# Keys split once per pair of heads and placed by DMA, query additions on GpSimd, in an attention and two-layer MLP kernel

## The chip, the cores and the metric

The kernel runs on one core of a Trainium2 chip. Such a core has five engines that run side by side, each with its own instruction queue that is worked off in order: TensorE (PE in the rows; its weight loads stand apart as PEld), VectorE (DVE), ScalarE (ACT), GpSimd (POOL) and SyncE (SP), which here issues every DMA transfer. The metric is the time of one execution in microseconds (us). A row of the profile that says L396 means line 396 of the kernel before.

## The reference, cut to what matters

```
q, k, v: (4, 8, 1152, 64) float32; w_in (512, 2048), w_out (2048, 512), a second pair likewise, float64
q_pool = q.reshape(B, H, S // 2, 2, D).mean(axis=3)
scores = q_pool @ k.T / sqrt(D);  scores -= max(scores, axis=-1)
attn = exp(scores);  attn /= sum(attn, axis=-1) + 1e-9
x = (attn @ v), heads side by side            # (2304, 512)
x = (h * cos(h)) @ w_out   with h = x @ w_in
out = elu(x @ w2_in) @ w2_out                 # (2304, 512) float32
```

## The kernel before, in words

**Exact products.** The kernel keeps float32's accuracy on a TensorE that rounds an operand of type float32r to 12 significant bits. An operand is split into hi (its rounding) and lo (what is left), and a product is made of several float32r products that accumulate in PSUM. Some products are done as plain float32 instead, which the trace records as two matmuls.

**Order of the work.** Attention goes over 16 pairs of heads (4 batches of 4 pairs). Head by head, `main_steps` (L429) makes 18 steps: 2 halves of 288 pooled queries by 9 blocks of 128 keys; so a pair has 36 steps. In a step, `s_step` (L438) makes the scores of one block by two matmuls (L442, L444) into one of three PSUM buffers `ps`, and ACT makes the exponentials `e` (L447, seven buffers). For 5 of the 9 key blocks (the tuple SPLIT) `halves` (L454) splits `e` one step later: hi is `eh` (a copy on ACT, L459, or on DVE, L457, in the first ten steps of the pair's first head), lo is `el` (a subtraction, L460, on GpSimd, and on DVE for steps 4 and 8 of the first head). Seven steps later (LAG) `v_step` (L464) multiplies by the values: three float32r matmuls (L475 to L477) for a split block, one float32 product (L479) for another. The values have 64 columns and a column of ones that gives the sum; their tiles `vt` and `vh` are 128 columns wide, the rest ones too.

**What is prepared for the next pair** while a pair is worked on, at steps that a hand-written plan fixes (L586 to L619):
- `add_q` (L319): five DVE additions pool the queries, steps 0 to 5. The squares (L308) that bound the rounding error are six ACT passes, steps 0 to 7.
- `q_group` (L323), at steps 4 and 6, and `k_group` (L347), at steps 8, 10 and 12: TensorE transposes (L332, L355) put both heads of the pair into one PSUM tile, head 0 on partitions 0 to 63 and head 1 on 64 to 127. One step later ACT copies each head's 64 partitions to hi (L337, L360), and two steps later DVE subtracts them to lo (L341, L364) and GpSimd copies hi once more (L343, L366). For the keys, hi goes to partitions 0 to 63 of `kst` of each head, lo to its partitions 64 to 127, and the second copy of hi to `k2`.
- `unit` (L383): from step 15 to 35, 27 units multiply the rounded queries by `kst` (L389, 384 keys at a time, through three PSUM buffers `big`), and DVE reduces each to its maximum (L396). `combine` (L398) and `spread` (L413) make the maxima that the score product then subtracts.
- Loads for the pair after (L250, step 12), values (L274, step 8; split at step 20 by L283), and decoding of the float64 weights, some 25 small tasks per pair on DVE, ACT and GpSimd (L117 to L132, far in the queues from one another), with a fetch and a store by DMA per half chunk.

Every engine takes its instructions in the order in which this plan writes them. In pairs 0 and 1 some units of the second head stand in other steps (L576 to L586). After attention come the two layers of the MLP (L647 on), which the change doesn't touch.

The ordering of one step, as the loop writes it:

```
s_step(i)
for t in due.pop(now[0], []): t()          # what later(steps, task) put off to this step
...                                        # v_step of seven steps ago
for t in plan.get(si, []): t()             # the plan's tasks of this step
```

Of the kernel before, what the change touches and what calls it, by code (L numbers as in the profile page):

```python
# [10 lines left out]
F32 = mybir.dt.float32  # L11
F32R = mybir.dt.float32r
# [18 lines left out]
EHV = 10  # L31
ELV = (4, 8)
# [3 lines left out]
def network(ctx, tc, q, k, v, w_in1, w_out1, w_in2, w_out2, out, ident, sq, exact):  # L36
    """Everything from inputs to output. The maxima that the softmax subtracts: from two exact
    products per score (exact), or from one that rounds the queries to 12 significant bits; sq then
    gets the sums of the squares of queries and keys, which bound what that rounding can do."""
# [20 lines left out]
    NM = 2 * NQB if exact else NQB  # L60

# [15 lines left out]
    # ------------------------------------------------- weights: float64 bits to hi + lo  # L77
# [8 lines left out]
    def decode_tasks(layer, f, half, dst):  # L86
        """Operations that bring half a chunk of weights (0: w_in, 1: w_out) into dst's hi and lo."""
# [78 lines left out]
    # ------------------------------------------------- blocks of tokens for the layers  # L166
# [52 lines left out]
    # ---------------------------------------------------------------- attention  # L219
    def attention():  # L220
# [5 lines left out]
        wd_p = att.enter_context(tc.tile_pool(name="wd", bufs=2))  # L226
        ps_big = att.enter_context(tc.tile_pool(name="ps_big", bufs=3, space=bass.MemoryType.PSUM))
# [6 lines left out]
        vhs = [apool.tile([P, 2 * NS, P], F32R, name=f"vh{i}") for i in range(2)]  # L234
        vls = [apool.tile([P, 2 * NS, D], F32R, name=f"vl{i}") for i in range(2)]
        for t in vts:
            nc.vector.memset(t[:, :, D:P], 1.0)
        for t in vhs:
            nc.gpsimd.memset(t[:, :, D:P].bitcast(F32), 1.0)
# [53 lines left out]
        def prep_tasks(n):  # L293
            kr, qr = raws.pop(n)
            qp = spool.tile([P, NQB, 2, D], F32, tag="qp", name=f"qp{n}")
# [12 lines left out]
            def square(i):  # L308
                x, m = (kr[:, 3 * i:3 * i + 3], P) if i < 3 else (qp[:, 2 * i - 6:min(2 * i - 4, NQB)], P)
                if i == 5:  # L310
                    m = SQ % P
                    x = x[0:m]
                junk = x_p.tile([P, KD, NB], F32, tag="xin", name=f"junk{n}_{i}")[:, 0, :].rearrange("p (c j d) -> p c j d", j=2, d=D)
                nc.scalar.activation(
                    junk[0:m, 0:x.shape[1]], x, AF.Square, accum_out=sq[0:m, i // 3, n, i % 3:i % 3 + 1])

            squares = [lambda i=i: square(i) for i in range(6)]
# [5 lines left out]
            def q_group(i0, i1):  # L323
                w = min(SQ, i1 * P) - i0 * P
                cols = [slice(j * OFF + i0 * P, j * OFF + i0 * P + w) for j in range(2)]
                ps = {}

                def put(pool=ps_big, tag="big"):
                    ps[0] = pool.tile([P, 512], F32, tag=tag, name=f"pq{n}_{i0}")
                    for i in range(i0, i1):  # L330
                        m = min(P, SQ - i * P)
                        nc.tensor.transpose(  # L332
                            ps[0][:, (i - i0) * P:(i - i0) * P + m],
                            qp[0:m, i].rearrange("p j d -> p (j d)"), ident[0:m, 0:m])

                def high(j):
                    nc.scalar.copy(qst[j][0:D, cols[j]], ps[0][j * D:(j + 1) * D, 0:w])  # L337

                def low(j):
                    hi = qst[j][0:D, cols[j]].bitcast(F32)  # L340
                    nc.vector.tensor_tensor(  # L341
                        q2[j][0:D, cols[j]], ps[0][j * D:(j + 1) * D, 0:w], hi, ALU.subtract)
                    nc.gpsimd.tensor_scalar(qst[j][D:P, cols[j]], hi, 1.0, 0.0, ALU.mult, ALU.add)  # L343

                return put, high, low

            def k_group(c0, c1):  # L347
                w = (c1 - c0) * P
                cols = slice(c0 * P, c1 * P)
                ps = {}  # L350

                def put():
                    ps[0] = ps_big.tile([P, 512], F32, tag="big", name=f"pk{n}_{c0}")
                    for c in range(c0, c1):
                        nc.tensor.transpose(  # L355
                            ps[0][:, (c - c0) * P:(c - c0 + 1) * P],
                            kr[:, c].rearrange("p j d -> p (j d)"), ident)

                def high(j):
                    nc.scalar.copy(kst[j][0:D, cols], ps[0][j * D:(j + 1) * D, 0:w])  # L360

                def low(j):
                    hi = kst[j][0:D, cols].bitcast(F32)
                    nc.vector.tensor_tensor(  # L364
                        kst[j][D:P, cols], ps[0][j * D:(j + 1) * D, 0:w], hi, ALU.subtract)
                    nc.gpsimd.tensor_scalar(k2[j][0:D, cols], hi, 1.0, 0.0, ALU.mult, ALU.add)  # L366

                return put, high, low

            adds = [lambda i=i: add_q(i) for i in range(NQB)]  # L370
            q_groups = [q_group(i, min(NQB, i + 3)) for i in range(0, NQB, 3)]
            k_groups = [k_group(c, c + NC // NU) for c in range(0, NC, NC // NU)]
            return adds, q_groups, k_groups, squares
# [55 lines left out]
        def main_steps(h):  # L429
# [8 lines left out]
            def s_step(i):  # L438
# [10 lines left out]
                if c in SPLIT:  # L449
                    eh = xs_p.tile([P, NB], F32R, tag="xh", name=f"eh{h}_{i}")[:, 0:HALF]  # L450
                    el = xs_p.tile([P, NB], F32R, tag="xl", name=f"el{h}_{i}")[:, 0:HALF]
                    es[i] = (eh, el)

                    def halves():  # L454
                        # The scalar engine has the next pair's copies in the first head's steps.
                        if j == 0 and i < EHV:
                            nc.vector.tensor_copy(eh, e)  # L457
                        else:
                            nc.scalar.copy(eh, e)  # L459
                        (nc.vector if j == 0 and i in ELV else nc.gpsimd).tensor_tensor(el, e, eh.bitcast(F32), ALU.subtract)  # L460

                    later(1, halves)

            def v_step(i):  # L464
# [6 lines left out]
                if c in SPLIT:  # L471
# [3 lines left out]
                    nc.tensor.matmul(acc[:, 0:HALF], vh, eh, start=first, stop=False)  # L475
                    nc.tensor.matmul(acc[0:D, 0:HALF], vl, eh, start=False, stop=False)  # L476
                    nc.tensor.matmul(acc[:, 0:HALF], vh, el, start=False, stop=last)  # L477
                else:
                    nc.tensor.matmul(  # L479
                        acc[:, 0:HALF], vt[:, j * NC + c, :], *e, start=first, stop=last)  # L480
# [43 lines left out]
        def group(g):  # L524
            put, high, low = g
            put()
            for j in range(2):
                later(1, lambda j=j: high(j))
                later(2, lambda j=j: low(j))
# [9 lines left out]
        for _, high, low in q_groups:  # L539
            high(0)  # L540
            low(0)
# [280 lines left out]
```

## Time and profile before

| | us |
|---|---|
| runs of the kernel before | 1426.86, 1427.74, 1429.59 |
| their median | 1427.74 |
| profiled execution, first to last instruction (span) | 1430.4 |
| of it ahead of the first step of attention | 15.1 |
| of it attention, to the last step | 594 |
| of it the MLP | 821 |

The page gives the profiled execution's span alone; no separate time for that execution is given, so its own time is at least 1430.4 us. A busy engine in a row is the union of its instructions' durations; a matmul's duration runs to its modelled end, so neighbouring matmuls overlap and a PE that shows as busy all the time can still be waiting a little. PEclk is the granted share of TensorE's clock: 1.00 is 2.4 GHz, 0.5 is 1.2 GHz.

### The profile page before, as it was taken

The page shows a single profiled execution, that of the slowest core. Times are in us where ns is not written, and L with a number is a line of the kernel's source. Part 1 is how long each engine was busy: PE and PEld are TensorE (multiplying, and loading weights), DVE is VectorE, ACT ScalarE, POOL GpSimd, SP SyncE. Part 2 cuts the span into 40 slices and gives each one's busy share as a digit, 9 for nine tenths or more (in the row PEclk, how much of TensorE's full clock was granted, in tenths as well). Part 3 has the DMA queues.
Part 4 walks back from the last instruction along what each step waited for, and adds up shares of the span by engine and source line. Part 5 has one row for each costly group of instructions (what it writes and reads, how often), then busy time and mean ns, then how long its engine had stood idle before and what let it go on. Part 6 is the DMA issues. An engine that isn't in the chain of part 4 may idle for free.

```text
span 1430.4 us, 22786 instructions
## 1 busy us (share of the span) xinstructions
PE 1368.7 (96%) x7683; PEld 1259.3 (88%) x7683; DVE 923.4 (65%) x1707; ACT 822.3 (57%) x2061; POOL 705.5 (49%) x849
## 2 busy tenths in 40 slices
PE   7998999999998999999999999999999999999997
PEld 5887888788887888899999999999999999999996
DVE  7789999999998999723888888887411111121111
ACT  5776777777776777655555555555633334343332
POOL 5657878777776787722222223232333333333332
PEclk8999999999999999999999999999999999999999
DMA  4232334445444443383525243439801010101000
GB/s 115 61 96 61 100 89 117 118 128 137 118 117 118 118 119 86 111 285 148 155 89 184 89 155 118 155 120 363 311 1 45 1 44 0 45 0 45 1 23 25
DMA packets 152542, 150.69 MB, mean 105 GB/s; under 512 B 81472, under 2 KB 129600, under 8 KB 152416
## 3 DMA queue, kind: packets, MB, share of 16 engines
q1 hardware_dynamic: 152416, 149.15, 34.4%
q8 instruction: 62, 1.02, 0.3%
q14 instruction: 64, 0.52, 0.1%
HBM read 105.46 MB, written 43.66 MB: 104 GB/s over the span
## 4 chain that ended last, share of the span: by engine, by line
PE 57%; issue 18%; DVE 15%; POOL 7%; ACT 2%; DMA 1%; SPq 0%; POOLq 0%; DVEq 0%; ACTq 0%
PE po L726 17%; PE ph L672 6%; PE ph L670 6%; PE ph L671 6%; POOL gl L702 6%; PE acc L479 5%; DVE mm L396 5%; PE pm L389 4%; PE ps L442 3%; PE ps L444 3%; PE acc L477 2%; PE acc L475 2%; PE acc L476 2%; DVE kst L364 1%; DVE e L128 1%
## 5 line engine op out<-in xcount | busy, mean ns | idle before, releaser
L702 POOL TENSOR_TENSOR gl<-u,gh 128x384 fp32r<-128x384 f32 x192 | 208.1, 1084 | 330.8 <-ACT gh L701 316.8
L460 POOL TENSOR_TENSOR el<-e,eh 128x288 fp32r<-128x288 f32 x288 | 253.1, 886 | 146.5 <-ACT eh L459 49.9
L447 ACT ACTIVATE e<-ps 128x288 f32<-128x288 f32 x576 | 234.2, 411 | 139.5 <-PE ps L444 97.7
L672 PE MATMUL ph<-xh,w 128*128 128x384 f32 x768 | 257.9, 336 | 0.0
L670 PE MATMUL ph<-xh,w 128*128 128x384 f32 x768 | 257.7, 336 | 0.0
L671 PE MATMUL ph<-xl,w 128*128 128x384 f32 x768 | 257.5, 335 | 0.0
L396 DVE TENSOR_REDUCE mm<-pm 128x1 f32<-128x384 f32 x432 | 221.3, 548 | 25.8 <-PE pm L389 24.6
L726 PE MATMUL po<-gh,w 128*128 128x384 f32 x768 | 211.5, 336 | 0.4 <-ACT gh L701 0.4
L389 PE MATMUL pm<-kst,qst 128*128 128x384 f32 x480 | 176.5, 415 | 27.6 <-DVE kst L364 15.4
L442 PE MATMUL ps<-qst,kst 128*128 128x288 f32 x576 | 197.1, 342 | 1.8 <-ACT e L447 1.8
L699 DVE SCALAR_TENSOR_TENSOR u<-ph,a 128x384 f32<-128x384 f32 x96 | 52.8, 554 | 225.7 <-POOL a L685 225.7
L726 PE MATMUL po<-w,gh 128*128 128x512 f32 x576 | 179.6, 393 | 0.0
L444 PE MATMUL ps<-q,k 69*128 69x288 f32 x576 | 174.3, 303 | 0.4 <-DVE q L418 0.4
L683 ACT ACTIVATE a<-ph 128x384 f32<-128x384 f32 x96 | 47.2, 492 | 213.9 <-PE ph L672 213.9
L479 PE MATMUL acc<-e,vt 128*128 128x288 f32 x512 | 169.4, 412 | 0.0
L701 ACT CAST gh<-u 128x384 fp32r<-128x384 f32 x192 | 97.4, 508 | 112.3 <-DVE u L696 86.9
L685 POOL TENSOR_SCALAR a<-a 128x384 f32<-128x384 f32 x96 | 49.4, 514 | 222.0 <-ACT a L684 222.0
L670 PEld LDWEIGHTS ph<-xh,w 128*128 128x128 f32 x768 | 144.2, 188 | 4.1
L671 PEld LDWEIGHTS ph<-xl,w 128*128 128x128 f32 x768 | 144.2, 188 | 3.9
L672 PEld LDWEIGHTS ph<-xh,w 128*128 128x128 f32 x768 | 144.2, 188 | 0.0
L389 PEld LDWEIGHTS pm<-kst,qst 128*128 128x128 f32 x480 | 90.3, 196 | 58.4 <-DVE mm L396 24.6
L726 PEld LDWEIGHTS po<-gh,w 128*128 128x128 f32 x768 | 140.2, 188 | 1.4 <-ACT gh L701 1.0
(87 smaller groups left out, 2779.0 us busy)
## 6 DMA issues: line engine op xcount, KB each, us to landing
w_d<-wd SPq DMA_DIRECT2D x56, 512.0 KB, 2.9
w<-w_d SPq DMA_DIRECT2D x56, 512.0 KB, 8.8
raw<-in_moe_w_in_dram SPq DMA_DIRECT2D x32, 512.0 KB, 5.3
raw<-in_moe_w_out_dram SPq DMA_DIRECT2D x32, 512.0 KB, 4.3
vt<-in_v_dram SPq DMA_DIRECT2D x32, 288.0 KB, 4.5
kr<-in_k_dram SPq DMA_DIRECT2D x30, 288.0 KB, 4.3
qr<-in_q_dram SPq DMA_DIRECT2D x32, 256.0 KB, 4.5
x_d<-xo SPq DMA_DIRECT2D x32, 144.0 KB, 2.3
```

The costliest lines, as they stand in the source:

```text
L389: nc.tensor.matmul(ps[:, 0:W], qst[:, i * P:(i + 1) * P], kst[:, u * W:(u + 1) * W], start=first, stop=last and not exact)
L396: nc.vector.reduce_max(mm[:, x, u:u + 1], ps[:, 0:W], axis=AX.X)
L442: nc.tensor.matmul(ps[:, 0:HALF], kst[:, c * P:(c + 1) * P], qst[:, qs], start=True, stop=False)
L444: nc.tensor.matmul(ps[:, 0:HALF], k2[0:KR, c * P:(c + 1) * P], q2[0:KR, qs], start=False, stop=True)
L447: nc.scalar.activation(e, ps[:, 0:HALF], AF.Exp, scale=SCALE)
L460: (nc.vector if j == 0 and i in ELV else nc.gpsimd).tensor_tensor(el, e, eh.bitcast(F32), ALU.subtract)
L479: nc.tensor.matmul(acc[:, 0:HALF], vt[:, j * NC + c, :], *e, start=first, stop=last)
L670: nc.tensor.matmul(h, wh, xh, start=(c == 0), stop=False)
L671: nc.tensor.matmul(h, wh, xl, start=False, stop=False)
L672: nc.tensor.matmul(h, wl, xh, start=False, stop=(c == KD - 1))
L702: nc.gpsimd.tensor_tensor(gl, u, gh.bitcast(F32), ALU.subtract)
L726: nc.tensor.matmul(o, a, b_, start=st and t == 0, stop=sp and t == 2)
```

## The change

The keys of pairs 1 to 15 are split once for both heads: ACT copies all 128 partitions of the transposed PSUM tile to a tile `uk`, DVE subtracts to `vk`, and ten DMA transfers per pair (64 partitions each) place the halves in `kst` and `k2` of the two heads; GpSimd's copies to `k2` go. Pair 0 keeps the old way but with both heads' copies ahead of the first step. The query additions go to GpSimd, in two instructions. The squares are three passes. All copies to `eh` are on ACT and all subtractions to `el` on GpSimd. The key groups stand at steps 0, 2 and 4, the query groups at 6 and 8, the transfers at steps 3 and 4 (first third of the keys, four transfers of 96 KB), 7 and 8 (the other two thirds, four of 192 KB) and 10 and 11 (`k2`, two of 288 KB), the load of the pair after at step 13. In pair 0 all of these stand seven steps later. The tiles of the values are 66 columns wide.

```
-        vts = [apool.tile([P, 2 * NC, P], F32, name=f"vt{i}") for i in range(2)]
+        vts = [apool.tile([P, 2 * NC, VW], F32, name=f"vt{i}") for i in range(2)]      # VW = D + 2
...
+            uk = upool.tile([P, S], F32R, tag="uk", name=f"uk{n}")
+            vk = upool.tile([P, S], F32R, tag="vk", name=f"vk{n}")
...
-                x, m = (kr[:, 3 * i:3 * i + 3], P) if i < 3 else (qp[:, 2 * i - 6:min(2 * i - 4, NQB)], P)
+                x, m = ((kr, P), (qp[:, 0:SQ // P], P), (qp[0:SQ % P, SQ // P:], SQ % P))[i]
...
-            def add_q(i):
-                m = min(P, SQ - i * P)
-                nc.vector.tensor_tensor(qp[0:m, i], qr[0:m, i, :, 0], qr[0:m, i, :, 1], ALU.add)
+            def add_q(i0, i1):
+                m = min(P, SQ - i0 * P)
+                nc.gpsimd.tensor_tensor(
+                    qp[0:m, i0:i1], qr[0:m, i0:i1, :, 0], qr[0:m, i0:i1, :, 1], ALU.add)
+
+            def place(dst, src):
+                nc.sync.dma_start(out=dst.bitcast(F32), in_=src.bitcast(F32))
...
+                def high():
+                    if n and tag == "k":
+                        nc.scalar.copy(uk[:, cols], ps[0][:, 0:w])
+                        return
+                    for j in range(2):
+                        dst = kst[j][0:D, cols] if tag == "k" else qst[j][0:D, j * OFF + c0:j * OFF + c0 + w]
+                        nc.scalar.copy(dst, ps[0][j * D:(j + 1) * D, 0:w])
+
+                def low():
+                    if n and tag == "k":
+                        nc.vector.tensor_tensor(vk[:, cols], ps[0][:, 0:w], uk[:, cols].bitcast(F32), ALU.subtract)
+                        return
+                    for j in range(2):
...
+                        nc.vector.tensor_tensor(lo, ps[0][j * D:(j + 1) * D, 0:w], hi.bitcast(F32), ALU.subtract)
+                        nc.gpsimd.tensor_scalar(again, hi.bitcast(F32), 1.0, 0.0, ALU.mult, ALU.add)
...
+            places = [
+                [lambda j=j, r=r, c=c: place(kst[j][halves[r], c], (uk, vk)[r][halves[j], c])
+                 for r in range(2) for j in range(2)] for c in (first, others)
+            ] + [[lambda j=j: place(k2[j][0:D, :], uk[halves[j], :]) for j in range(2)]] if n else []
...
                     def halves():
-                        # The scalar engine has the next pair's copies in the first head's steps.
-                        if j == 0 and i < EHV:
-                            nc.vector.tensor_copy(eh, e)
-                        else:
-                            nc.scalar.copy(eh, e)
-                        (nc.vector if j == 0 and i in ELV else nc.gpsimd).tensor_tensor(el, e, eh.bitcast(F32), ALU.subtract)
+                        nc.scalar.copy(eh, e)
+                        nc.gpsimd.tensor_tensor(el, e, eh.bitcast(F32), ALU.subtract)
...
-                    nc.tensor.matmul(acc[:, 0:HALF], vh, eh, start=first, stop=False)
+                    nc.tensor.matmul(acc[0:VW, 0:HALF], vh, eh, start=first, stop=False)
...
         for _, high, low in q_groups:
-            high(0)
-            low(0)
+            high()
+            low()
...
-                spread_over(d, d + 5, adds)
+                spread_over(d, d + 2, adds)
...
-                    at(d + 12, lambda: load(n + 2))
-                for x, g in enumerate(q_groups):
-                    at(d + 4 + 2 * x, lambda g=g: group(g))
-                for x, g in enumerate(k_groups):
-                    at(d + 8 + 2 * x, lambda g=g: group(g))
+                    at(d + 13, lambda: load(n + 2))
+                for x, g in enumerate(k_groups + q_groups):
+                    at(d + 2 * x, lambda g=g: group(g))
+                for x, step in enumerate((3, 7, 10)):
+                    spread_over(d + step, d + step + 2, places[x])
```

## Rows read from the trace of the kernel before

**Rows 1.** The page: busy time, share of the span and instructions of each engine.
```profile
PE 1368.7 (96%) x7683; PEld 1259.3 (88%) x7683; DVE 923.4 (65%) x1707; ACT 822.3 (57%) x2061; POOL 705.5 (49%) x849
```
**Rows 2.** Windows (busy time of each engine in a stretch): pairs 2 to 13, pair 15.
```profile
core 0: us, PE busy (x) PEld busy (x) DVE busy (x) ACT busy (x) POOL busy (x), PEclk, DMA share, GB/s
...
92.35:542.50 450.15, 416.96 (x2523) 368.38 (x2521) 422.00 (x823) 333.38 (x965) 346.88 (x417) 0.98 0.42 113
...
580.20:609.26 29.06, 27.28 (x166) 24.15 (x165) 17.76 (x31) 20.70 (x58) 21.86 (x22) 0.94 0.17 53
```
**Rows 3.** Windows over steps 0 to 6 of pairs 2 to 13: fastest, sum.
```profile
133.77:139.75 5.98, 5.98 (x40) 5.24 (x39) 5.60 (x16) 5.50 (x20) 4.05 (x5) 1.00 0.03 9
...
sum 82.68, PE 75.55 PEld 63.33 DVE 80.42 ACT 70.07 POOL 59.04; mean PE 6.30 PEld 5.28 DVE 6.70 ACT 5.84 POOL 4.92
```
**Rows 4.** Windows over steps 7 to 14 of the same pairs: sum.
```profile
sum 79.28, PE 79.25 PEld 72.63 DVE 74.40 ACT 75.41 POOL 57.21; mean PE 6.60 PEld 6.05 DVE 6.20 ACT 6.28 POOL 4.77
```
**Rows 5.** Windows over steps 15 to 21 of the same pairs: two pairs, sum.
```profile
221.22:230.13 8.91, 7.99 (x47) 6.85 (x45) 8.49 (x17) 5.14 (x16) 8.78 (x11) 1.00 0.99 243
...
330.99:339.35 8.36, 7.71 (x47) 6.70 (x45) 7.55 (x14) 4.79 (x14) 8.30 (x11) 1.00 0.62 153
...
sum 120.12, PE 101.12 PEld 85.88 DVE 109.47 ACT 75.66 POOL 108.49; mean PE 8.43 PEld 7.16 DVE 9.12 ACT 6.30 POOL 9.04
```
**Rows 6.** Windows over steps 22 to 35 of the same pairs: fastest, sum.
```profile
230.13:242.98 12.85, 12.85 (x85) 12.16 (x84) 12.16 (x25) 10.03 (x29) 11.40 (x13) 1.00 0.28 91
...
sum 168.07, PE 161.04 PEld 146.54 DVE 157.70 ACT 112.24 POOL 122.14; mean PE 13.42 PEld 12.21 DVE 13.14 ACT 9.35 POOL 10.18
```
**Rows 7.** Waits in pairs 2 to 13: us in total, times, longest us.
```profile
ACT e L447 <- POOL el L460: 25.3, 27, 2.0
...
PEld pm L389 <- DVE mm L396: 20.8, 32, 2.8
...
PE pm L389 <- DVE kst L364: 12.2, 15, 2.0
PEld pq L332 <- DVE qp L321: 10.1, 13, 1.7
```
**Rows 8.** Groups by line and shape: count, busy us, mean ns, idle before.
```profile
L460 POOL TENSOR_TENSOR el<-e,eh 128x288 fp32r<-128x288 f32 x288 | 253.1, 886 | 146.5 <-ACT eh L459 49.9 <-DVE eh L457 44.3 <-PE ps L444 26.3
...
L459 ACT CAST eh<-e 128x288 fp32r<-128x288 f32 x224 | 95.3, 425 | 0.0
...
L364 DVE TENSOR_TENSOR kst<-pk,kst 64x384 fp32r<-64x384 f32 x96 | 53.2, 556 | 7.1 <-ACT kst L360 4.8
...
L366 POOL TENSOR_SCALAR k<-kst 64x384 fp32r<-64x384 f32 x96 | 49.8, 532 | 3.4 <-ACT kst L360 2.5
...
L360 ACT CAST kst<-pk 64x384 fp32r<-64x384 f32 x96 | 45.0, 471 | 2.3 <-PE pk L355 1.2
...
L457 DVE CAST eh<-e 128x288 fp32r<-128x288 f32 x96 | 43.4, 452 | 0.5
...
L130 POOL TENSOR_TENSOR m<-m,wd 128x512 f32<-128x512 f32 x24 | 33.0, 1377 | 0.2
...
L321 DVE TENSOR_TENSOR qp<-qr 128x128 f32<-128x128 f32 x64 | 24.6, 396 | 1.9 <-DMA qr<-in_q_dram 1.8
...
L460 DVE TENSOR_TENSOR el<-e,eh 128x288 fp32r<-128x288 f32 x32 | 20.6, 644 | 1.1
```
**Rows 9.** Timeline of DVE ahead of the first steps: start us, us, instructions merged.
```profile
16.97 1.51 DVE L364 TENSOR_TENSOR kst<-pk,kst 64x384 fp32r<-64x384 f32 x3
```
**Rows 10.** Timeline of SP in pair 8 (one transfer's issue), and times to landing.
```profile
326.00 0.50 SPq L486 DMA_DIRECT2D x_d<-xo  x1
...
w<-w_d SPq DMA_DIRECT2D x56, 512.0 KB, 8.8
...
x_d<-xo SPq DMA_DIRECT2D x32, 144.0 KB, 2.3
```
**Rows 11.** Waits of SP's queue in pairs 2 to 13: total, times, longest.
```profile
SPq L152 <- POOL wd L131: 84.2, 18, 7.8
```

More of the change, by code (lines that the diff above doesn't have):

```diff
@@ L30 @@
 SV = 20
-EHV = 10
-ELV = (4, 8)
 @with_exitstack
@@ L60, in network @@
     NM = 2 * NQB if exact else NQB
+    VW = D + 2
     wpool = ctx.enter_context(tc.tile_pool(name="wpool", bufs=NPREW))
@@ L226, in attention @@
         wd_p = att.enter_context(tc.tile_pool(name="wd", bufs=2))
+        upool = att.enter_context(tc.tile_pool(name="upool", bufs=1))
         ps_big = att.enter_context(tc.tile_pool(name="ps_big", bufs=3, space=bass.MemoryType.PSUM))
@@ L229, in attention @@
         ps_a = att.enter_context(tc.tile_pool(name="ps_a", bufs=2, space=bass.MemoryType.PSUM))
-        vts = [apool.tile([P, 2 * NC, P], F32, name=f"vt{i}") for i in range(2)]
+        vts = [apool.tile([P, 2 * NC, VW], F32, name=f"vt{i}") for i in range(2)]
         k2s = [apool.tile([P, S], F32R, name=f"k2_{i}") for i in range(4)]
         qsts = [apool.tile([P, NQB * P], F32R, name=f"qst{i}") for i in range(4)]
-        vhs = [apool.tile([P, 2 * NS, P], F32R, name=f"vh{i}") for i in range(2)]
+        vhs = [apool.tile([P, 2 * NS, VW], F32R, name=f"vh{i}") for i in range(2)]
         vls = [apool.tile([P, 2 * NS, D], F32R, name=f"vl{i}") for i in range(2)]
         for t in vts:
-            nc.vector.memset(t[:, :, D:P], 1.0)
+            nc.vector.memset(t[:, :, D:VW], 1.0)
         for t in vhs:
-            nc.gpsimd.memset(t[:, :, D:P].bitcast(F32), 1.0)
+            nc.gpsimd.memset(t[:, :, D:VW].bitcast(F32), 1.0)
         for t in k2s:
@@ L317, in prep_tasks @@
-            squares = [lambda i=i: square(i) for i in range(6)]
-            def add_q(i):
-                m = min(P, SQ - i * P)
-                nc.vector.tensor_tensor(qp[0:m, i], qr[0:m, i, :, 0], qr[0:m, i, :, 1], ALU.add)
-            def q_group(i0, i1):
-                w = min(SQ, i1 * P) - i0 * P
-                cols = [slice(j * OFF + i0 * P, j * OFF + i0 * P + w) for j in range(2)]
+                x, m = ((kr, P), (qp[:, 0:SQ // P], P), (qp[0:SQ % P, SQ // P:], SQ % P))[i]
+                if not m:
+                    return
@@ new lines, in square @@
+                junk = x_p.tile([P, KD, NB], F32, tag="xin", name=f"junk{n}_{i}").rearrange("p c n -> p (c n)")
+                junk = junk[0:m, 0:x.shape[1] * 2 * D].rearrange("p (c j d) -> p c j d", j=2, d=D)
+                nc.scalar.activation(
+                    junk, x, AF.Square, accum_out=sq[0:m, min(i, 1), n, i // 2:i // 2 + 1])
+            squares = [lambda i=i: square(i) for i in range(3)]
+            def add_q(i0, i1):
+                m = min(P, SQ - i0 * P)
+                nc.gpsimd.tensor_tensor(
+                    qp[0:m, i0:i1], qr[0:m, i0:i1, :, 0], qr[0:m, i0:i1, :, 1], ALU.add)
@@ L326, in q_group, with group, put @@
+            def place(dst, src):
+                nc.sync.dma_start(out=dst.bitcast(F32), in_=src.bitcast(F32))
+            def group(src, blocks, w, tag):
                 ps = {}
[L328 to L331, printed above, removed]
+                def put(pool=ps_big, t="big"):
+                    ps[0] = pool.tile([P, 512], F32, tag=t, name=f"p{tag}{n}_{blocks[0]}")
+                    for x, i in enumerate(blocks):
+                        m = min(P, w - x * P)
@@ L345, in q_group @@
-                return put, high, low
[L347 to L373, printed above, removed]
+                            ps[0][:, x * P:x * P + m],
+                            src[0:m, i].rearrange("p j d -> p (j d)"), ident[0:m, 0:m])
+                c0 = blocks[0] * P
+                cols = slice(c0, c0 + w)
@@ new lines, in high @@
+                def high():
[8 more added lines that the diff above has]
+                        nc.vector.tensor_tensor(vk[:, cols], ps[0][:, 0:w], uk[:, cols].bitcast(F32), ALU.subtract)
+                        return
+                    for j in range(2):
+                        qc = slice(j * OFF + c0, j * OFF + c0 + w)
+                        hi, lo, again = (
+                            (kst[j][0:D, cols], kst[j][D:P, cols], k2[j][0:D, cols]) if tag == "k"
+                            else (qst[j][0:D, qc], q2[j][0:D, qc], qst[j][D:P, qc]))
+                        nc.vector.tensor_tensor(lo, ps[0][j * D:(j + 1) * D, 0:w], hi.bitcast(F32), ALU.subtract)
+                        nc.gpsimd.tensor_scalar(again, hi.bitcast(F32), 1.0, 0.0, ALU.mult, ALU.add)
@@ new lines, in group @@
+                return put, high, low
+            halves = [slice(j * D, (j + 1) * D) for j in range(2)]
+            step = NC // NU
+            first, others = slice(0, step * P), slice(step * P, S)
+            places = [
+                [lambda j=j, r=r, c=c: place(kst[j][halves[r], c], (uk, vk)[r][halves[j], c])
+                 for r in range(2) for j in range(2)] for c in (first, others)
+            ] + [[lambda j=j: place(k2[j][0:D, :], uk[halves[j], :]) for j in range(2)]] if n else []
@@ L375, in max_tasks @@
+            nfull = SQ // P
+            adds = [lambda: add_q(0, nfull)]
+            if SQ % P:
+                adds.append(lambda: add_q(nfull, NQB))
+            q_groups = [
+                group(qp, list(range(i, min(NQB, i + 3))), min(SQ, (i + 3) * P) - i * P, "q")
+                for i in range(0, NQB, 3)]
+            k_groups = [group(kr, list(range(c, c + step)), step * P, "k") for c in range(0, NC, step)]
+            return adds, q_groups, k_groups, squares, places
         def max_tasks(n):
@@ L474, in v_step @@
                     vh, vl = vhs[h // 2 % 2][:, ci], vls[h // 2 % 2][:, ci]
-                    nc.tensor.matmul(acc[:, 0:HALF], vh, eh, start=first, stop=False)
+                    nc.tensor.matmul(acc[0:VW, 0:HALF], vh, eh, start=first, stop=False)
                     nc.tensor.matmul(acc[0:D, 0:HALF], vl, eh, start=False, stop=False)
-                    nc.tensor.matmul(acc[:, 0:HALF], vh, el, start=False, stop=last)
+                    nc.tensor.matmul(acc[0:VW, 0:HALF], vh, el, start=False, stop=last)
                 else:
                     nc.tensor.matmul(
-                        acc[:, 0:HALF], vt[:, j * NC + c, :], *e, start=first, stop=last)
+                        acc[0:VW, 0:HALF], vt[:, j * NC + c, :], *e, start=first, stop=last)
                 if c == NC - 1:
@@ L526, in group @@
             put()
-            for j in range(2):
-                later(1, lambda j=j: high(j))
-                later(2, lambda j=j: low(j))
+            later(1, high)
+            later(2, low)
         load(0)
         load_v(0)
-        adds, q_groups, k_groups, squares = prep_tasks(0)
+        adds, q_groups, k_groups, squares, places = prep_tasks(0)
         units, combine, spread = max_tasks(0)
@@ L539, in attention @@
         for _, high, low in q_groups:
-            high(0)
-            low(0)
+            high()
+            low()
         for put, high, low in k_groups:
             put()
-            high(0)
-            low(0)
+            high()
+            low()
         split_v(0)
@@ L550, in attention @@
             t()
-        for _, high, _ in q_groups + k_groups:
-            high(1)
         combine(0, 0, HB)
         spread(0, 0, HB, ps_s, "s")
-        for _, _, low in q_groups + k_groups:
-            low(1)
         if not exact:
```

18 lines of the change are left out of this document (2 added, 16 removed).

## The prediction

> **What bounds the kernel now.** The page's first part shows PE busy for 96% of the span [rows 1], but a matmul's duration runs to a modelled end, so that share hides waits. The useful view is windows by stretch. The MLP's instructions are not changed; I read only attention. Pairs 2 to 13 take 450.15 us, 37.5 us each, with DVE busy 422.00 of it, the largest share of any engine [rows 2]. DVE is thus the first suspect.
>
> I cut each of the twelve pairs at steps 0, 7, 15 and 22 (the start of the step's first score matmul L442) and divide each sum by 12. That gives 6.89 us for steps 0 to 6, 6.61 for 7 to 14, 10.01 for 15 to 21 and 14.01 for 22 to 35 [rows 3 to 6]. The reader should see that they don't have the same limit. Over steps 7 to 14 PE is busy 79.25 of 79.28 us: it sets the pace there and nothing that the change takes from DVE can shorten it [rows 4]. The fastest pair's steps 0 to 6 (5.98 us) and steps 22 to 35 (12.85 us) are busy on PE throughout too, so these are PE's own times [rows 3, 6]. Steps 15 to 21 are the odd ones: 10.01 us with PE busy 8.43, DVE 9.12 and POOL 9.04 [rows 5]. Their own PE time I estimate from the count of matmuls: 46 against 84 in the 12.85 us, so 46/84 x 12.85 = 7.04 us [rows 5, 6]. The floor of a pair is then 5.98 + 6.61 + 7.04 + 12.85 = 32.5 us, and 5.0 us of each pair is waiting: 0.9, 0, 3.0 and 1.2 us by stretch.
>
> The waits say for what [rows 7]. In steps 15 to 21 the maxima's matmuls wait for the keys' lo (12.2 us over the twelve pairs) and for DVE's reductions to free their PSUM buffers (20.8). ACT's exponentials wait for a buffer `e` that GpSimd's `el` still reads (25.3). In steps 0 to 6 the transposes of the queries wait for DVE's additions (10.1). All are queues: DVE and POOL come to step 15 behind the plan and catch up there, while PE stands.
>
> **The change, part by part, for one pair.**
>
> DVE loses five additions (5 x 0.396 = 1.98 us), half of the keys' subtractions (six of 64 partitions become three of 128; a row is 384 elements long either way, so 3 x 0.556 = 1.67), six copies to `eh` (6 x 0.452 = 2.71) and two `el` (2 x 0.644 = 1.29): 7.65 us of durations [rows 8]. Some of a duration overlaps the next instruction: three key subtractions in a row took 1.51 us, 0.50 each, not 0.556 [rows 9]. I take about 6 of DVE's 35.2 us. All of it stands ahead of step 15, so DVE gets to its first reduction without a backlog. What then is late next is PE itself.
>
> ACT gains the six copies (6 x 0.425 = 2.55) and loses three of six key copies (3 x 0.471 = 1.41) [rows 8]; three of the six square passes go as well, which I count as nothing. At most 1.1 us more, on an engine busy 5.84 of 6.89 us in steps 0 to 6, and 6.28 of 6.61 after [rows 3, 4]. It has two or three score buffers of slack, and I charge 0.4 us of PE waiting in steps 0 to 6 for it.
>
> GpSimd loses six copies of `k2` (6 x 0.532 = 3.19) and gains two `el` (2 x 0.886 = 1.77) and the additions. The large one has 512 elements per partition and two inputs, as L130 has: 1.38 us. The small one, 64 partitions of 128 elements, is bounded by nothing below and by `el`'s 0.886 above; I take 0.5, as the shorter length leads me to. In all +0.46 us [rows 8]. In steps 0 to 21 it was busy 4.92 + 4.77 + 9.04 = 18.7 of 23.5 us [rows 3 to 5]; now 19.2. Its additions come at steps 0 and 1, where it was idle 2 us of 6.89, and the transposes that read them stand only at step 6, so PE's wait for additions goes. Queued behind the additions are `el` of the pair's first steps; each has six steps before a matmul reads it.
>
> Ten transfers per pair are added, 4 x 96 + 4 x 192 + 2 x 288 = 1728 KB. The nearest row, 64 partitions and 144 KB out of SBUF, takes 0.50 us of SP to issue and lands in 2.3 us; the worst row of a crowded queue is 8.8 us for 512 KB [rows 10]. The first third is issued at step 3 for a use at step 15, the rest at 7 and 8 for a use near step 19 (five of 27 units into a stretch of 20 steps). From step 8 to 19 there are some 7/8 x 6.6 + 4 = 9.8 us. Against it stand 4 x 0.50 of issue and 2.3 to 8.8 of flight, 4.3 to 10.8. I take a value near the lower end, because that row is the nearest in kind, and charge nothing; the cover gone, each us too late is a us of PE. The ten are ahead of the load of the pair after in SP's queue, which thus lands some us later, for a use 20 steps on. What SP is moved past are the stores and fetches of the weights' decoding, each with its next use about a decoding round away. DVE's subtraction is what SP waits for at each group of transfers, and behind it stand only `xo`'s stores and the values' load, due at step 20.
>
> The narrower value tiles cost or bring nothing: a matmul streams the same 288 columns, and over steps 7 to 14 PE is paced by matmuls, not by weight loads (72.63 of 79.28 us) [rows 4].
>
> The prologue gets longer: ten copies and ten subtractions instead of five and five come before the first maxima. Five more subtractions at 0.50 [rows 9] are 2.5 us; the bounds are 0 (ACT and DVE hide each other) and 5 x 0.556 = 2.8. The same work is taken out of pair 0, where I count it as nothing, since that pair's stalls are in the sum below.
>
> So a pair becomes, by stretch: 6.3 (5.98 and 0.3 to 0.4 for ACT), 6.6, 7.7 (of 3.0 us of waiting 0.7 stay, for decoding that still comes in clumps) and 13.3 (half of 1.2 goes, being backlog of the stretch before). That is 33.9 us, 3.6 less than 37.5. Fifteen pairs prepare a next one: 15 x 3.6 = 54 us. Less 2.5 for the prologue, 51.5 us go: the span 1430.4 becomes 1378.9. The profiled execution's span lies 2.7 us above the median of the runs, so against the median the time is 1427.7 - 51.5 = **1376 us**. What a measurement of this kernel can tell from no change is 0.2%, 2.9 us.
>
> A half clock (0.84 to 0.87 in some stretches) comes after PE has stood. Its cost is inside the sums above.
>
> **Rivals.**
>
> *GpSimd takes DVE's place.* With 19.2 us to do in steps 0 to 21, and the forecast's 20.6 us for them, it would be busy 93% of the time, against 80% now and 90% in the stretch where it queues [rows 3 to 5]. If it can't be fed more closely than now, steps 0 to 21 stay at 23.5 us, the wait of ACT for `el` grows, and only steps 22 to 35 gain: 15 x 0.7 - 2.5 = 8 us, so 1420. Half way is 1398. Against it: in steps 0 to 14 it idles because DVE makes `eh` late, and these now come from ACT in step; and a lag of six steps costs nothing. The Trainium skill's page "GPSIMD Engine Reference", section "Performance versus the Vector engine", is against such a move: two-input elementwise work runs about half as fast there as on VectorE. The row is milder, 886 against 644 ns for `el` [rows 8]. By the page's ratio two `el` and additions would be 2 x 1.29 + 2 x 1.98 = 6.5 us instead of 3.65, an estimate; that would make this rival the likeliest. The rows decide for me.
>
> *The transfers come late (slower than before).* Place: the units from step 15, which now wait for a DMA. Price: each us past the slack of 9.8 us is a us of PE in each of 15 pairs, and 3.6 us of lateness eat the gain. SP's queue can stand for up to 7.8 us at a store that waits for GpSimd's decoding [rows 11], and the DMA engines are at 0.99 in one pair's steps 15 to 21 [rows 5]. With 8.8 us of flight, 2 of issue and 7.8 of standing, 18.6 in all, a pair would be late by 8.8 and lose 5.2 net: 1430 + 78 + 2.5 = 1508 with all at its worst; at half that lateness 4.4 us, 0.8 net, 1442. I price it at 1450. It decides where transfers land over 13.4 us after step 8. Against it: standing for a store means waiting in an idle queue, mostly ahead of need, and the DMA share is 0.42 over these pairs [rows 2].
>
> *Nothing moves.* PE keeps waiting, since ACT at 1.1 us more stands where DVE stood: its 12.1 busy us of 13.5 in steps 0 to 14 [rows 3, 4] become 13.2, and the backlog is carried on to step 15 as now. The time is 1428.
>
> **How the numbers follow.** Forecast 0.66, GpSimd 0.18, late transfers 0.08, nothing 0.05, and 0.03 for a slower result by a cause not seen here. Nearly all of the chance for a gain lies with the first two, so faster by over 0.2% has 0.85, within 0.2% 0.05, slower 0.10. The forecast's own range runs from all 5.0 us of each pair, 15 x 5.0 = 75 and no prologue, 1353, to two fifths of the gain lost, 1396. The range goes on to 1404, into the upper half of the GpSimd case.
>
> **What would show it.** Steps 15 to 21 below 8.5 us on average, with PE's waits for `kst` and for DVE's additions near nothing; DVE busy near 29 us of a pair and not the busiest engine; POOL at about 27 us of 34. Waits of ACT for `el` growing above 25 us would speak for GpSimd; waits of L389 for a DMA for the transfers; steps 15 to 21 still at 10 us with ACT late for nothing. The forecast is wrong if pairs 2 to 13 take over 36 or under 32.5 us each.

## The result, and the profile after

The changed kernel takes 1413.24 us (median of 4 runs, 1413.20 to 1414.32) against 1427.3 for the kernel before (4 runs, 1423.41 to 1429.59): a ratio of 0.990, 95% interval 0.9875 to 0.9926. It is faster, by 14 us; forecast were 52, and the time lies above the range given (1353 to 1404). The profiled execution of the changed kernel took 1413.25 us with a span of 1411.4; its span is 19 us below that of the kernel before, whose profiled execution was longer than the median of its runs.

The page, busy time of each engine:

```profile
PE 1360.6 (96%) x7683; PEld 1239.2 (88%) x7683; DVE 809.9 (57%) x1454; ACT 818.9 (58%) x2016; POOL 703.9 (50%) x823
```

Windows of the changed kernel, cut as in [rows 2 to 6]: the prologue, pairs 2 to 13, the last pair (to its last step); then over those twelve pairs steps 0 to 6 (the fastest, and the sum) and the sums of steps 7 to 14, 15 to 21 and 22 to 35.

```profile
0.00:19.29 19.29, 7.78 (x24) 5.25 (x25) 9.83 (x23) 8.72 (x19) 13.06 (x31) 1.00 0.67 158
...
93.96:526.57 432.61, 411.67 (x2522) 354.14 (x2521) 332.21 (x631) 330.13 (x929) 342.63 (x393) 0.98 0.70 166
...
562.13:590.01 27.88, 25.92 (x165) 22.08 (x164) 15.08 (x23) 22.26 (x64) 23.57 (x24) 1.00 0.16 52
...
491.53:497.99 6.46, 6.46 (x47) 5.82 (x46) 5.18 (x10) 6.06 (x19) 5.38 (x6) 1.00 0.42 120
...
sum 77.79, PE 77.79 PEld 69.98 DVE 52.42 ACT 72.95 POOL 66.87; mean PE 6.48 PEld 5.83 DVE 4.37 ACT 6.08 POOL 5.57
...
sum 79.01, PE 77.23 PEld 59.90 DVE 48.44 ACT 77.61 POOL 64.85; mean PE 6.44 PEld 4.99 DVE 4.04 ACT 6.47 POOL 5.40
...
sum 112.31, PE 97.47 PEld 83.32 DVE 79.52 ACT 71.53 POOL 96.78; mean PE 8.12 PEld 6.94 DVE 6.63 ACT 5.96 POOL 8.07
...
sum 163.50, PE 159.18 PEld 140.93 DVE 151.83 ACT 108.05 POOL 114.12; mean PE 13.27 PEld 11.74 DVE 12.65 ACT 9.00 POOL 9.51
```

DVE did what was expected of it: 27.7 us of a pair instead of 35.2, and no longer the busiest engine. But a pair went only from 37.5 to 36.05 us. The stretch that was to give most, steps 15 to 21, went from 10.01 to 9.36. The DMA share of the twelve pairs rose from 0.42 to 0.70 [rows 2].

The mean hides the pattern. Windows over pairs 7, 8 and 11, over steps 15 to 21 of pair 7, and over the end of these, from the moment when TensorE goes on after a stop:

```profile
269.57:310.67 41.10, 36.20 (x213) 31.20 (x211) 27.84 (x52) 27.25 (x79) 28.18 (x34) 0.92 0.67 146
310.67:345.61 34.94, 33.77 (x213) 29.11 (x211) 27.75 (x55) 27.22 (x78) 28.88 (x34) 1.00 0.74 182
416.24:456.85 40.61, 36.33 (x212) 31.32 (x211) 27.93 (x53) 27.67 (x78) 28.35 (x33) 0.92 0.63 147
...
282.23:296.97 14.74, 10.21 (x46) 8.60 (x45) 6.76 (x12) 6.20 (x18) 9.69 (x13) 0.77 1.18 219
...
291.26:296.97 5.71, 5.71 (x19) 4.96 (x20) 2.14 (x4) 2.58 (x7) 3.67 (x5) 0.54 1.18 218
```

Two pairs take 41 us; the other ten take (432.6 - 81.7)/10 = 35.1 each. In the long ones the granted clock over steps 15 to 21 is 0.77 (pair 7) and 0.76 (pair 11): after PE had stood it ran for a while mostly at the lower of its two levels, 1.2 GHz (0.54 over the 5.7 us behind the stop of pair 7). The waits of pairs 2 to 13 (us in total, times, longest) name the place:

```profile
PEld pm L400 <- DVE mm L407: 17.5, 34, 2.1
ACT e L458 <- POOL el L467: 16.2, 21, 2.1
...
PEld pm L400 <- issue: 9.1, 2, 4.8
DVE m L118 <- POOL w L130: 5.8, 3, 4.1
...
PE pm L400 <- issue: 4.5, 1, 4.5
PE pm L400 <- DMA kst<-vk: 4.4, 2, 4.1
```

The waits of the maxima's matmuls for DVE's subtraction (12.2 us in [rows 7]) are gone, as are the transposes' for DVE's additions. New are two stops of over 4 us, one in pair 7 and one in pair 11, each ahead of the first unit that reads the second third of the keys. For pair 11 the profile names the transfers `kst<-vk` (4.1); for pair 7 it names nothing ("issue", 4.5). That the lo transfers hold pair 7 too is read from the same place in the plan, and from the runs below in which both stops go together. New is also a wait of DVE for GpSimd's decoding of weights, 4.1 us at most, which is in pair 3. SP's queue in pair 7 (start us, length, issue; x2 is two transfers) shows what stood before them, and TensorE's timeline the stop:

```profile
279.12 0.58 SPq L109 DMA_DIRECT2D raw<-in_moe_w_in_dram  x1
279.74 1.22 SPq L328 DMA_DIRECT2D kst<-uk  x2
281.01 2.05 SPq L278 DMA_DIRECT2D vt<-in_v_dram  x2
283.16 4.16 SPq L328 DMA_DIRECT2D kst<-vk  x2
287.37 1.23 SPq L328 DMA_DIRECT2D k<-uk  x2
```

```profile
286.44 0.29 PE L484 MATMUL acc<-el,vh 128*66 128x288 f32 x1
291.26 0.66 PE L400 MATMUL pm<-kst,qst 128*128 128x384 f32 x1 [4.53 <-issue]
```

A weight fetch of 512 KB, two transfers for the keys' hi, then the values' load for the next pair, and only then the two transfers of lo. They are issued 13.6 us after the pair's start and need 4.16 us to issue where two others need 1.2 (the first of them alone 3.52; in pair 11 it is 2.25), and TensorE goes on 8.1 us after their issue began.

### The profile page after: what moved, and what is told of

Its sections match the earlier page's. It is cut to its first block, busy times and chain, and to the rows that moved or that the text cites. A ratio compares the mean times of both kernels' runs of the same rounds, so it can differ in the third digit from the quotient of the medians.

```text
span 1411.4 us, 22684 instructions
## 1 busy us (share of the span) xinstructions
PE 1360.6 (96%) x7683; PEld 1239.2 (88%) x7683; DVE 809.9 (57%) x1454; ACT 818.9 (58%) x2016; POOL 703.9 (50%) x823
## 4 chain that ended last, share of the span: by engine, by line
PE 67%; issue 14%; DVE 7%; POOL 6%; DMA 2%; ACT 2%; SPq 1%; POOLq 0%; DVEq 0%; ACTq 0%
PE po L728 20%; PE ph L674 7%; PE ph L672 7%; PE ph L673 7%; PE acc L486 6%; POOL gl L704 5%; PE ps L453 4%; PE pm L400 4%; PE ps L455 4%; DVE mm L407 3%; PE acc L482 2%; PE acc L483 2%; PE acc L484 2%; DMA kst<-vk 1%; PE pk L339 1%
## 5 line engine op out<-in xcount | busy, mean ns | idle before, releaser
L467 POOL TENSOR_TENSOR el<-e,eh 128x288 fp32r<-128x288 f32 x320 | 274.1, 863 | 136.6 <-ACT eh L466 92.7
L400 PE MATMUL pm<-kst,qst 128*128 128x384 f32 x480 | 172.3, 412 | 20.3 <-DVE mm L407 8.0
L486 PE MATMUL acc<-e,vt 128*66 128x288 f32 x512 | 167.9, 409 | 0.0
L466 ACT CAST eh<-e 128x288 fp32r<-128x288 f32 x320 | 137.4, 429 | 0.0
```

The source lines that it names most:

```text
L400: nc.tensor.matmul(ps[:, 0:W], qst[:, i * P:(i + 1) * P], kst[:, u * W:(u + 1) * W], start=first, stop=last and not exact)
L467: nc.gpsimd.tensor_tensor(el, e, eh.bitcast(F32), ALU.subtract)
L486: nc.tensor.matmul(acc[0:VW, 0:HALF], vt[:, j * NC + c, :], *e, start=first, stop=last)
```

## The experiments

Twelve kernels. "Changed" is the kernel after. The times of the kernel before, beside the three sets of runs, were 1427.1, 1428.6 and 1427.2 us.

**The values' load behind the transfers.**

```
-                at(LAG + 1, lambda: load_v(n + 1))
+                at(LAG + 5, lambda: load_v(n + 1))
```

> The changed kernel with the values' load for the next pair at step 12 instead of step 8, so that all transfers of the keys' lo halves stand ahead of it in SP's queue. Theory A (the lo halves come late behind the values' load: pairs 7 and 11 took 41.1 and 40.6 us against 35.0 for the others, with a half clock behind it): both pairs come down to about 35 us, 10 to 12 us less in all, 1402. Rival B (GpSimd paces the pairs, the late transfers are only where it shows): the two pairs stay over 39 us, 1411 to 1414. Rival C (DMA traffic as a whole is too much): another transfer is late in their place, and the time does not change by over 3 us.

Measured: 1411.89 us (1409.38 to 1413.98). Pairs 7 and 11 came down to 37.0 and 36.0 us, but pairs 6, 10 and 14 went from 34.7, 35.7 and 35.6 to 37.6, 39.8 and 37.1. In pairs 2 to 13 a wait took the old one's place:

```profile
ACT vh L287 <- DMA vt<-in_v_dram: 17.8, 10, 4.4
```

The load now lands too late for the split at step 20, ACT stops there, and with it the exponentials. So theory A held for pairs 7 and 11, where the load's place in the queue was the cause, and rival C held for the time: the lateness went to the next load in line that was needed soon. Rival B did not hold.

**And its split later.** The same, with

```
-SV = 20
+SV = 30
```

> The changed kernel with the values' load at step 12 (as in the run with the values later) and their split at step 30 instead of 20, so that ACT does not wait for the load. Theory A (what is late is whichever load stands behind the transfers in SP's queue, and it matters only as it has a use soon after): no pair over 38 us, pairs 6, 7, 10 and 11 near 35, 1398 to 1402. Rival C (the DMA traffic as a whole is too much): some pairs stay at 37 to 40 us and the time within 3 us of 1412.

Measured: 1399.02 us (1397.93 to 1399.75), 14.2 less than the changed kernel. No pair from 4 on is over 35.4 us, and both stops are gone. Pair 3 took 38.6 us, over the 38 that theory A allowed, but it is as long in the kernels without transfers (see the other terms below). SP's queue in pair 7 of this kernel:

```profile
281.09 1.22 SPq L328 DMA_DIRECT2D kst<-uk  x2
282.41 1.36 SPq L328 DMA_DIRECT2D kst<-vk  x2
283.81 1.33 SPq L328 DMA_DIRECT2D k<-uk  x2
285.19 2.35 SPq L278 DMA_DIRECT2D vt<-in_v_dram  x2
287.59 4.10 SPq L257 DMA_DIRECT2D qr<-in_q_dram  x1
```

The 4 us stand is still there, behind the values' load as before, but it now falls on the load of the pair after, which nobody needs for 20 steps. The DMA share of pairs 2 to 13 is the same (0.71):

```profile
93.07:513.81 420.74, 407.78 (x2523) 351.26 (x2521) 335.08 (x631) 329.57 (x929) 342.80 (x393) 1.00 0.71 171
```

So it was not the amount of traffic that cost the 14 us, but its order. The two moves together could have been a gain of their own; two controls ask that.

**The kernel before with both moves** (`LAG + 5` for the values' load, `SV = 30`).

> The kernel before with the same two moves as in the run with values and split later (load at step 12, split at step 30), nothing else. If those moves only undo what the ten transfers bring about, the time stays within 4 us of the kernel before; if they are a gain of their own (the split's work taken out of the crowded steps 15 to 21), it falls by 8 us or more.

Measured: 1434.00 us (1431.15 to 1441.54), a ratio of 1.0049 (1.0032 to 1.0067). Not a gain of its own: 7 us slower, more than the 4 allowed for.

**The changed kernel with the split alone later** (`SV = 30`, the load as it was).

> The changed kernel with the split at step 30 and the load left at step 8. Theory A (the values' load ahead of the lo halves in SP's queue is the cause): pairs 7 and 11 stay over 39 us and the time within 3 us of 1413. If the split's work in the crowded stretch was the cause: near 1399.

Measured: 1415.57 us (1413.46 to 1418.93); pairs 7 and 11 take 40.9 and 41.2 us. The split's place is not the cause; the load's is. The gain needs both moves, though: the load behind the transfers, and the split late enough not to wait for it.

**The additions back on DVE.**

```
-                nc.gpsimd.tensor_tensor(
+                nc.vector.tensor_tensor(
                     qp[0:m, i0:i1], qr[0:m, i0:i1, :, 0], qr[0:m, i0:i1, :, 1], ALU.add)
```

> The changed kernel with the query additions (two instructions) back on DVE. GpSimd has about 1.7 us less to do per pair, DVE about 1.0 to 1.3 us more. Theory A (late transfers hold the time): the ordinary pairs stay near 35.0 us, total within 4 us of 1413. Rival B (GpSimd paces the ordinary pairs through the buffers of e): 1 us less per pair, 15 us in all, 1398, and ACT's waits for el go down from 16 us in pairs 2 to 13. Rival D (DVE still paces): 1 us more per pair, 1425 or more.

Measured: 1407.64 us (1406.69 to 1410.19), 5.6 less than the changed kernel, between the theories' figures and outside the 4 us of theory A. In the profiled execution, the slowest of the four, the two long pairs stay long (40.2 and 39.5) and the ten ordinary ones stay at 35.2 (35.1 before the edit), as theory A has it; ACT's waits for `el` fell from 16.2 to 13.7 us. The prologue is 1.4 us shorter, pair 0 1.1 and the two long pairs 2.0 together. Moving the additions to GpSimd was a loss all the same.

**The same with the late loads out of the way** (values and split later, additions on DVE).

> The run before in this call with the query additions on DVE too. With the late loads out of the way, theory B (GpSimd paces ordinary pairs) has 0.5 to 1 us per pair less, 7 to 15 us, and 1.4 us of prologue; the theory that GpSimd's additions are covered has the prologue's 1.4 us and no more than 3 us in all.

Measured: 1391.40 us (1389.88 to 1393.70), 7.6 less than without the additions' move. The prologue is 1.5 us shorter, and pairs 2 to 13 take 416.2 us instead of 420.7, 0.4 each, with GpSimd at 27.2 us of a pair instead of 28.6:

```profile
91.60:507.77 416.17, 404.82 (x2523) 351.96 (x2521) 339.91 (x655) 328.26 (x929) 325.87 (x369) 1.00 0.71 173
```

That would fit a GpSimd that paces a little, but 0.4 us a pair is just under the 0.5 that theory B asked for. This is the fastest of all the kernels, at 0.973 (0.971 to 0.9753) of the kernel before; only the last variant below, at 1391.83, can't be told from it.

**The halves of the exponentials as before.** Six copies and two subtractions per pair on DVE again.

```
-                        nc.scalar.copy(eh, e)
-                        nc.gpsimd.tensor_tensor(el, e, eh.bitcast(F32), ALU.subtract)
+                        if j == 0 and i < 10:
+                            nc.vector.tensor_copy(eh, e)
+                        else:
+                            nc.scalar.copy(eh, e)
+                        (nc.vector if j == 0 and i in (4, 8) else nc.gpsimd).tensor_tensor(el, e, eh.bitcast(F32), ALU.subtract)
```

> The changed kernel with the halves of the exponentials shared out as before: six copies to eh and two subtractions per pair on DVE. ACT has about 2.0 us less per pair, GpSimd 1.6 us less, DVE 2.3 us more. Rival B (GpSimd paces): 1 us less per pair, about 1400. Rival E (ACT paces steps 0 to 6): steps 0 to 6 go from 6.48 us to 6.0, 7 us in all, 1406. Theory A and rival D (DVE paces): 1413 to 1425, steps 15 to 21 longer than 9.4 us on average.

Measured: 1410.76 us (1410.08 to 1415.26), not to be told from the changed kernel. Steps 7 to 14 of the ten ordinary pairs fell from 6.6 to 6.2 us on average (6.0 in most), steps 15 to 21 rose from 8.3 to 8.7: the two sides cancel. Steps 0 to 6, which rival E expected to fall, stayed at 6.5.

> As the run before, with the halves of the exponentials shared out as before the change too (six copies and two subtractions on DVE). If DVE still had a share in the pace, steps 15 to 21 get longer by 0.5 us or more and the time rises by 7 us; if ACT or GpSimd paces the first half of a pair, steps 7 to 14 go from 6.6 to 6.1 us and the time falls by 5 to 8 us; the sum of both may come out at nothing.

The same on the fastest kernel. Measured: 1399.24 us (1398.68 to 1400.74), 7.8 more. Steps 7 to 14 again gained (6.4 to 6.0 us on average), steps 15 to 21 lost 0.5 and steps 0 to 6 0.1, and pairs 0 and 1 lost 2.1 us together. Moving the halves off DVE was a gain, once nothing else was late.

**The keys by the engines, no transfers.**

```
-                    if n and tag == "k":
+                    if False:
...
-                for x, step in enumerate((3, 7, 10)):
+                for x, step in enumerate((3, 7, 10) if places else ()):
```

> The changed kernel with the keys of every pair split per head by the engines as before (six copies on ACT, six subtractions on DVE, six copies to k2 on GpSimd) and without the ten transfers; order and steps as in the changed kernel. DVE has 1.7 us, ACT 1.4 us, GpSimd 3.2 us more per pair. Theory A (the transfers cost about as much as they save): within 5 us of 1413, with no pair over 39 us. Rivals B, D, E (an engine paces): 1.5 to 3 us more per pair, 1435 to 1458.

Measured: 1426.31 us (1424.17 to 1427.40), 13 us more than the changed kernel and no different from the kernel before (0.9986, 0.9970 to 1.0002). No pair over 39 us, but ordinary ones at 37 instead of 35. The time is outside both forecasts (within 5 us of 1413, or 1435 and more). So all parts of the change other than the keys come to nothing in sum, and the keys' part brought the whole gain, late transfers included.

> The fastest kernel so far (values and split later, additions on DVE, 1391.4) with the keys split per head by the engines and without the ten transfers. What the keys' part is worth once nothing is late: the changed kernel against its run with keys by the engines had 13 us. If the late transfers hid a part of it, it is now 20 us or more, 1412 or over; if the engines' extra work is covered by other waits, 1400 or less.

On the fastest kernel: 1421.12 us (1419.61 to 1421.77), 29.7 more. That is what the keys' part is worth with no transfer late, against 13 before: the late transfers and the additions' place had hidden over half of it. A part of the 29.7 may belong to the two moves of the values, which stayed in this run and cost the kernel before 7 us; no run has the keys by the engines without them and with the additions on DVE.

**The first pair's order.** Second head's copies and subtractions behind the first maxima, as before; first on the kernel with values and split later, then on the fastest.

```
...
-            high()
-            low()
+            high((0,))
+            low((0,))
...
+        for _, high, _ in q_groups + k_groups:
+            high((1,))
...
+        for _, _, low in q_groups + k_groups:
+            low((1,))
```

> The first run of this call with the first pair's copies and subtractions in the old order, the second head's behind the first maxima. The prologue, 19.3 us in the changed kernel against 15.1 before, should come down by 2.5 us of the 4.2 (the rest is the additions on GpSimd); if the work is only put off into pair 0, that pair gets longer by as much and the time stays.

> The same fastest kernel with the first pair's second head behind the first maxima. Prologue down by 2.5 us, pair 0 longer by 1 to 2.5: 1389 to 1391.5.

Measured: 1397.67 us (1396.73 to 1397.88) against 1399.02, and 1391.83 (1390.16 to 1396.46) against 1391.40. The prologue fell by 2.7 and 2.4 us and pair 0 grew by 1.6 and 1.5: mostly put off, worth 1.4 us at best.

## Why the prediction was wrong

**What bounds the kernel** was read rightly in the main. Steps 15 to 21 were a queue behind DVE and GpSimd: with DVE relieved they came down from 9.7 to 8.3 us in the ten ordinary pairs (the prediction's sign was an average under 8.5 over all). No pair of any kernel went under the floor of 32.5 us (the shortest was 33.2; the last pair, which prepares nothing, is left out), and steps 0 to 6 and 7 to 14 of the changed kernel have PE busy for 77.79 of 77.79 and 77.23 of 79.01 us. The floor's parts moved, though: the keys' transposes now stand in steps 0 to 6 (47 matmuls in the fastest window where there were 40 [rows 3]), which take 6.5 us of PE's own time, and steps 7 to 14 need only 6.0 (their time on the fastest kernel with the halves of the exponentials back on DVE).

**The step that failed** is the transfers, charged with nothing. The cover was sized rightly: the prediction has 9.8 us from step 8 to the use, and in six of the ten ordinary pairs the first unit that reads the late part starts 10.2 to 10.5 us after step 8, in the others later. What stands against the cover, "4.3 to 10.8" us of issue and flight, was sized too small. Of SP's queue the prediction says that behind DVE's subtraction, which each group of transfers waits for, "stand only `xo`'s stores and the values' load, due at step 20"; it left out that the plan puts the values' load between the two hi and the two lo transfers of steps 7 and 8. In pairs 7 and 11 the issue of the lo transfers began 6.4 and 6.8 us after step 8 and took 4.2 and 2.9 us, and TensorE went on 14.5 and 14.1 us after step 8. In the other pairs that unit started 3.2 to 6.0 us after the issue of lo had ended, against 3.9 and 4.4 in the two that waited: by this estimate most pairs had little or nothing to spare (pair 14 waited 0.7 us). In pairs 7 and 11 TensorE stopped and its clock fell. A weight fetch of 512 KB stood ahead in the queue there, 9.6 and 9.0 us after the pair's start; pairs 2 and 4 had one at the same place in the queue, but at 6.2 and 6.1 us, and did not stop. The fetch's part in it was not tested by itself.

The two pairs are 41.1 + 40.6 - 2 x 33.9 = 13.9 us over the forecast, and the run with values and split later got back 14.2. The rival of late transfers had the right mechanism and the right sign, a wait of the units for a DMA; its mark of 13.4 us after step 8 was passed in these two pairs. But it saw the lateness in all pairs or none and asked for a queue that stands at a store; it was a matter of two pairs in fifteen, behind a load. (Its worst case is added up as 1430 + 78 + 2.5 = 1508; that is 1510.5, and 1508 only from the median of 1427.7.) The trace of the kernel before had shown such a stand already. There, in pair 7, the queries' load behind a weight fetch and the values' load took 2.3 us to issue:

```profile
289.67 0.54 SPq L110 DMA_DIRECT2D raw<-in_moe_w_in_dram  x1
290.30 1.36 SPq L278 DMA_DIRECT2D vt<-in_v_dram  x2
291.76 2.33 SPq L257 DMA_DIRECT2D qr<-in_q_dram  x1
```

**The other terms.** The forecast had 33.9 us for an ordinary pair; the ten have 35.1, together 12 us over. By stretch they took 6.5, 6.6, 8.3 and 13.6 us where 6.3, 6.6, 7.7 and 13.3 were forecast, so over half of the 12 stands in steps 15 to 21.

Some of it may be the additions. The two runs that moved them back gained 5.6 and 7.6 us in all, prologue included; the second gained 0.4 us a pair, the first nothing in ordinary pairs. The forecast called PE's wait for them covered, which it was; it counted their 1.88 us of GpSimd as free, and that did not hold. The page "GPSIMD Engine Reference" of the Trainium skill advises in its section "Engine selection" against two-input elementwise work there, as about 2 times slower than on VectorE. The runs side with the advice, though not with the factor: on the kernel before `el` took 886 against 644 ns [rows 8], and the two additions took 1.88 us on GpSimd in the changed kernel against 1.23 on DVE in the run with them moved back.

Pair 3 alone is 3.2 of the 12 us over. It took 37.1 to 39.3 us in the changed kernel and every variant of it, with or without transfers (35.3 before). DVE stands there for up to 4.1 us at a decoding task until GpSimd has made `w`, and the reductions behind it in DVE's queue wait as well. No run took that wait away, so this is read from the trace and not shown.

For the rest, the waits of ACT for `el` (16.2 us, down from the 25.3 of [rows 7]) and of the weight loads for DVE's reductions (17.5 after 20.8) are what the trace names; which of them leads was not settled.

Pairs 0, 1 and 14 were given 3.6 us each like the others and gained 2.2, 0.3 and 2.1, 6 us short. In pairs 0 and 1 more of the time is TensorE's own: it is busy for 35.8 and 36.0 us of them in the changed kernel, against 33.8 in pair 8.

The prologue grew by 4.2 us (15.1 to 19.3) instead of 2.5; the row behind the difference is the start of the additions on GpSimd, which TensorE waits 7.4 us for at the start (5.6 before). With the additions back on DVE the prologue was 1.4 us shorter.

13.9 + 12 + 6 + 1.7 = 33.6 us; with 1.2 us that the last pair gained, unforeseen, that is the 32 us between the forecast's 51.5 and the 19 by which the spans differ. The runs differ by only 14, as the profiled execution of before was slower than its median.

**What else held, and where.** ACT's extra work was charged with 0.4 us in steps 0 to 6. These are all PE's; a cost of that size shows in steps 7 to 14 instead. There ACT is the busiest engine (77.61 of 79.01 us), and with the halves of the exponentials back on DVE these steps fell by 0.4 us on average on both kernels. That edit takes work from GpSimd too, so ACT's share of the 0.4 is not shown apart. The narrower values changed nothing that can be seen in matmuls of 288 columns: after a matmul of `eh` with 66 columns the next starts 0.13 us later, as after the others.

## What to carry to other kernels

A transfer has a place in its queue like an instruction has on an engine: before work is handed to DMA, write down what the plan puts ahead of it in that queue, with the issue time of each, and what stands between its landing and its first use. Where the queue is busy, put the transfers that are needed soon first and the loads with 20 steps to spare last. Here that order, with the split moved to suit it, was worth 14 us at the same amount of traffic. And look at the distribution of a stretch before its mean: two pairs of fifteen held nearly all of what was lost to lateness.

## What the runs showed of the hardware that was not expected

The issue of a transfer on SP is not a fixed cost. A transfer of 64 partitions mostly took 0.5 to 0.6 us to issue. The issue that came next behind the values' load (two times 288 KB in pieces of 256 bytes) took 0.8 to 1.4 us in most pairs of the changed kernel and 3.5 and 2.3 us in pairs 7 and 11 (`kst<-vk`), and 4.1 us in pair 7 of the kernel with values and split later (`qr`): it was long whichever transfer stood there. In these timelines nothing behind it on SP starts while it stands.

The DMA share in steps 15 to 21 was shown as 1.04 to 1.18 in pairs 2 to 13, above one, where it was at most 0.99 before. The added transfers, which go from SBUF to SBUF, are not the only cause: with the keys by the engines and no such transfers it still reached 1.19 in one pair (pair 10). How a share above one comes about stays open.
